# Batch 1's first units scored in one slot each, the values behind the products, and the first output tile summed in another PSUM bank

## The chip, the cores and the metric

The kernel runs on one core of one Trainium2 chip. The metric is device time in microseconds, the median of several executions. Four engines matter here: TensorE (PE) multiplies, with its weight loads (PEld) beside it; ScalarE (ACT) does exponentials and copies; VectorE (DVE) does element-wise work; GpSimd (POOL) does some clamping and issues the loads. SyncE (SP) issues the stores.

## The reference

For 8 batches and 8 heads of 576 positions with head size 64, sliding-window attention with a position bias is computed. The heads of a position are joined to a row of 512. Two matrix products follow, with an ELU between them. Only what fixes the work is kept here:

```python
scores = scale * np.matmul(q, k.transpose(0, 1, 3, 2))
bias = slopes[:, None, None] * (-np.abs(rel))[None]      # rel = query - key position
mask = (rel >= 0) & (rel < 128)
attn = softmax(np.where(mask, scores + bias, -1e9))
x = np.matmul(attn, v).transpose(0, 2, 1, 3).reshape(4608, 512)
h = x @ w_in                                             # 512 -> 2048
g = np.where(h > 0, h, np.exp(np.minimum(h, 0)) - 1)
out = g @ w_out                                          # 2048 -> 512
```

## The kernel before, in words

**One program order, written by hand.** Python lists say what is issued in which *slot*; the loop at the end walks the slots and issues everything, and each engine runs its own part strictly in that order. Within slot `s` the order is: `early`, then the hidden-layer chunk `HID[s]`, then the ELU's last step (`elu`) of the chunk of slot `s - 1`, then the `tasks` of the slot (put there by `at`, or at their head by `at_once`), then the output work `OUT[s]`, then `late` (put there by `after`). A task of `at` thus stands between the hidden chunk and the output products of its slot; one of `after` stands behind the products.

**Attention.** A batch is cut into four units of 128 keys (`u`), and a unit into two halves of four heads. For batches 0 and 1 a half goes through `first_scores` (line 176: four matmuls of 64 rows by 128 columns of the array, 256 wide, two running side by side), `first_expo` (ScalarE, lines 205 and 210), for batch 1 `first_weigh` (VectorE, line 216, the bias and mask as a factor), and later `values` (line 253: the attention times v, then on VectorE a reciprocal `rden`, line 259, and a product `xn`, line 260). `turn` (line 289) transposes `xn` on TensorE and copies it into `xT`, which the hidden layer reads. `turn_first` (line 136) transposes the loaded q and k of a batch into `QT` and `KT`; the loads are those of `s` (line 101). From batch 2 on other functions do this (lines 225 to 285).

**Hidden layer.** A chunk is 16 matmuls of 128 columns (line 305, 32 of 64 columns in some) into a bank `hp0`, `hp1` or `sp2`; then ScalarE takes the exponential (line 315, followed by GpSimd at 316; or lines 312 and 313 on ScalarE alone), and `elu` (VectorE, line 323, `g`) writes `g` and frees the bank.

**Output.** The first 256 rows are summed plainly by `output` (line 329, four 512-wide matmuls per call, four calls per tile of 128 rows; ScalarE copies the sum out at line 336). All later rows go by a scheme of seven products per pair of tiles (`product`, line 393, 256-wide matmuls, 7 or so per slot), with VectorE's `sums` and `combine` (line 354) before and after. For the first pair the products 1, 6, 7 and 4 are summed in bank `op`, and 2, 5 and 3 in `sp3`. `combine(1, "C11")` adds product 2, straight out of `sp3`, to a kept copy of product 1; product 5 then starts over in `sp3`.

**PSUM.** There are eight banks: `sp0` and `sp1` (together `spa`), `sp2`, `sp3`, `hp0`, `hp1`, `av`, `op`. In `first_scores` the argument `d` names a pair of them: `pairs[0]` is `spa`, `pairs[2]` is `hp0` with `hp1`.

```python
for s in range(min(slots), max(slots) + 1):
    for f, a in early.get(s, []):
        f(*a)
    for step in HID.get(s, []):
        hidden(*step, s in SOFT)
    if s - 1 in HID and s not in (1, 4, 5):
        done(s - 1)
    for f, a in tasks.get(s, []):
        f(*a)
    for f, a in OUT.get(s, []):
        f(*a)
    for f, a in late.get(s, []):
        f(*a)
```

Of the kernel before, what the change touches and what calls it, by code (L numbers as in the profile page):

```python
# [18 lines left out]
def kernel(  # L19
# [9 lines left out]
    nc = tc.nc  # L29
# [47 lines left out]
    sp = [spa[:, 0, :], spa[:, 1, :]] + [ps_s.tile([128, 512], F32, name=f"sp{i}", tag=f"sp{i}") for i in (2, 3)]  # L77
    hp = [ps_h.tile([128, 512], F32, name=f"hp{i}", tag=f"hp{i}") for i in range(2)]
    av = ps_v.tile([128, 512], F32, name="av", tag="av")
    op = ps_o.tile([128, 512], F32, name="op", tag="op")  # L80
# [68 lines left out]
    with tc.manual_schedule():  # L149
# [348 lines left out]
        early, tasks, late, HID, OUT = {}, {}, {}, {}, {}  # L498

        def at(s, f, *a):  # L500
            tasks.setdefault(s, []).append((f, a))

        def at_once(s, f, *a):
            tasks.setdefault(s, []).insert(0, (f, a))

        def after(s, f, *a):
            late.setdefault(s, []).append((f, a))
# [23 lines left out]
        for o in range(16 * NTB):  # L531
            t, ts, f = o // 16, o // 4 % 4, o % 4
            if o // 8 in SEVEN:
                continue
            s = (9, 11, 13, 14)[o] if o < 4 else 11 + o if o < 13 else 2 * o - 1 if o < 16 else 15 + o
            OUT[s] = [(output, (t, ts, 4 * f, op))]

        def done(r):
            for step in HID[r]:
# [25 lines left out]
        at(5, first_scores, 0, 3, 1, 0)  # L565
        at(5, first_expo, 0, 3, 1, 0, 0, 256)
        at(5, done, 4)
        at(9, values, 0, 3, 0)
        at(9, values, 0, 3, 1, sp[3])
        at(10, values, 0, 4, 0)  # L570
        at(10, turn, 0, 3, nc.scalar.copy, sp[3])
        at(11, values, 0, 4, 1)
# [12 lines left out]
        at(16, turn_first, 1, 1, 0, 1, sp[3], nc.scalar.copy)  # L585
        at(17, turn_first, 1, 0, 0, 0, hp[1], nc.scalar.copy)
        at(17, turn_first, 1, 0, 0, 1, av, V.tensor_copy)
        at(19, turn_first, 1, 0, 1, 0, av, nc.scalar.copy)
        for u, a0, a1, d in ((0, 18, 19, 2), (1, 20, 21, 2), (2, 22, 24, 0), (3, 26, 28, 0)):
            for half, a in enumerate((a0, a1)):  # L590
                at(a, first_scores, 1, u, half, d * half)
                at(a, first_expo, 1, u, half, d * half, 0, 256)
                at(a + 1, first_weigh, 1, u, half)
                at(a + 2, values, 1, u, half, av if half else sp[2])
            at(a1 + 3 + u // 3, turn, 1, u, nc.scalar.copy, (av, av, av, sp[3])[u])
        at(25, turn_first, 1, 1, 1, 0, av, nc.scalar.copy)
        at(30, values, 1, 4, 0, sp[2])
        at(31, values, 1, 4, 1)
        at(32, turn, 1, 4)
# [6 lines left out]
        for b in range(2, B):  # L606
            for u in range(4):
                a = START[b] + 4 * u
# [11 lines left out]
            a = START[b - 1] if b > 2 else 0  # L620
# [17 lines left out]
        for n in SEVEN:  # L638
            s = 15 + 8 * n
            ps = (19, 20, 21, 22, 23, 25, 27, 29, 30) if n == 1 else range(s, s + 9)  # L640
            if n < 2 * NTB - 1:
                for d, i in ((-1, 1), (1, 2), (3, 3), (4, 4)):
                    (at_once if n > 2 else at)(ps[d] if d > 0 else ps[0] - 1, sums, n, i)
                after(ps[2], combine, n, "C11")
                after(ps[6], combine, n, "C12")
                (at_once if n > 2 else at)(ps[8], combine, n, "C22")
                for d in range(8):
                    OUT[ps[d]] = [(product, (n, i, j, j + 1)) for i, j in turns[7 * d:7 * d + 7]]
            else:
                at_once(s - 3, sums, n, 3)  # L650
                for i in (2, 1):
                    at_once(s - 2, sums, n, i, 0, 6)
                    at_once(s - 1, sums, n, i, 6, 8)
                at(s - 1, product, n, 1)
                OUT[s] = [(product, (n, 2)), (combine, (n, "C11")), (sums, (n, 4)), (product, (n, 6)), (product, (n, 5))]
                OUT[s + 1] = [(product, (n, 7)), (product, (n, 3)), (combine, (n, "C22")), (combine, (n, "C12")),
                              (last_out, (n,))]
# [48 lines left out]
```

## Time and profile before

| | |
|---|---|
| median of three runs | 310.42 us (310.11 to 310.88) |
| profiled execution | 310.72 us, of which the span is 308.9 us |
| granted TensorE clock | 1.00 |
| busy over the span | PE 97%, PEld 83%, DVE 84%, ACT 78%, POOL 35% |
| mean of a 16-matmul hidden chunk, start to start | about 0.89 us |
| `values` half, first unit (4 matmuls) | about 0.11 us |
| line 216 (`first_weigh`) | 0.68 to 0.69 us on DVE |
| line 205 (both banks of `spa`) | 1.02 us on ACT |

The span is from the first instruction to the last; the rest of the 310.72 us lies around it. In a timeline a row gives the start in the span, the duration, the engine, the line, the operation and what is written and read; in brackets stands the engine's idle time before it and what ended that. The rows of TensorE overlap[...]: the time that a group really took is read from one group's start to the next one's start. The slots that the change touches lie between 28 and 70 us.

### The profile page before, as it was taken

How to read it: one execution, taken by the hardware profiler on the slowest of the kernel's cores; microseconds unless marked ns; L12 is line 12 of the kernel's file. 1: busy time of each engine (PE TensorE's matmuls, PEld its weight loads, DVE VectorE, ACT ScalarE, POOL GpSimd, SP SyncE). 2: the span in 40 equal slices, each digit the busy share in tenths (PEclk: the TensorE clock that was granted, in tenths of full speed). 3: DMA queues.
4: the chain of work that ended last, by engine and by line, in shares of the span. 5: the costliest groups of instructions: out<-in, count | busy, mean ns of one | idle time of the engine just before them, and what ended most of it. 6: DMA issues, size and time to landing. Idle time of an engine off the chain costs nothing.

```text
span 308.9 us, 9842 instructions
## 1 busy us (share of the span) xinstructions
PE 300.8 (97%) x4079; PEld 256.5 (83%) x4079; DVE 258.0 (84%) x499; ACT 241.5 (78%) x445; POOL 108.5 (35%) x163
## 2 busy tenths in 40 slices
PE   7899999999999999999999999999999999999996
PEld 5688775798788888988888888888899888888885
DVE  5646887988989999997989998989998788886783
ACT  4576678778889698879797889788988797968881
POOL 8938868274261415140707060806000101010000
PEclk9999999999999999999999999999999999999999
DMA  9999999999197929495979997999620302030103
GB/s 95 188 198 201 201 176 189 92 118 122 23 153 73 152 55 149 55 142 70 109 93 118 130 98 82 125 135 107 68 92 15 96 17 87 19 97 1 70 17 121
DMA packets 96941, 32.04 MB, mean 104 GB/s; under 512 B 83968, under 2 KB 92800, under 8 KB 96896
## 3 DMA queue, kind: packets, MB, share of 16 engines
q0 software_dynamic: 75920, 18.36, 64.8%
q1 hardware_dynamic: 20832, 12.98, 17.4%
q8 instruction: 32, 0.52, 0.7%
q14 instruction: 13, 0.11, 0.1%
q10 hardware_dynamic: 144, 0.07, 0.1%
HBM read 36.70 MB, written 9.44 MB: 149 GB/s over the span
## 4 chain that ended last, share of the span: by engine, by line
PE 76%; DVE 7%; ACT 6%; DMA 5%; issue 3%; POOL 2%; POOLq 0%; DVEq 0%; ACTq 0%
PE hp L305 34%; PE op L393 13%; PE av L393 12%; PE spa L225 4%; PE spa L271 3%; DVE g L323 2%; DMA s<-in_q_dram 2%; DMA VP<-in_v_dram 2%; ACT EX L236 2%; PE op L329 1%; DMA xT<-xn 1%; PE sp L393 1%; POOL e L316 1%; PE sp L305 1%; ACT e L315 1%
## 5 line engine op out<-in xcount | busy, mean ns | idle before, releaser
L305 PE MATMUL hp<-xT,wi 128*128 128x256 f16 (+3 forms) x1488 | 144.2, 245 | 1.2 <-DVE g L323 0.5
L305 PEld LDWEIGHTS <-wi 128*128 128x128 f16 x1600 | 119.7, 98 | 18.2 <-issue 6.1
L323 DVE SCALAR_TENSOR_TENSOR g<-e,hp 128x512 f16<-128x512 f32 x138 | 93.7, 679 | 22.2 <-ACT e L313 12.7
L316 POOL TENSOR_SCALAR e<-e 128x512 f32<-128x512 f32 x44 | 28.0, 635 | 158.9 <-ACT e L315 153.4
L312 ACT ACTIVATE e<-hp 128x512 f32<-128x512 f32 x98 | 58.6, 598 | 28.8 <-PE hp L305 24.3
L313 ACT ACTIVATE e<-e 128x512 f32<-128x512 f32 x100 | 63.1, 631 | 3.2
L393 PEld LDWEIGHTS <-S 128*128 128x128 f16 x544 | 51.2, 98 | 6.8 <-issue 0.6
L393 PEld LDWEIGHTS <-g 128*128 128x128 f16 x400 | 37.4, 98 | 4.6 <-issue 0.6
L241 DVE TENSOR_TENSOR EX<-EX,TAB 128x1024 f16<-128x1024 f16 x48 | 32.9, 686 | 6.1 <-ACT EX L236 4.0
L114 POOL DMA_DIRECT2D VP<-in_v_dram x40 | 34.3, 870 | 0.8 <-PE hp L305 0.3
L315 ACT ACTIVATE e<-hp 128x512 f32<-128x512 f32 x40 | 24.1, 601 | 10.6 <-PE hp L305 10.6
L393 PE MATMUL op<-T,S 128*128 128x256 f16 x200 | 30.0, 273 | 0.1
L233 ACT ACTIVATE EX<-spa 128x1024 f16<-128x1024 f32 x24 | 24.6, 1025 | 3.7 <-PE spa L225 3.4
L393 PE MATMUL av<-T,S 128*128 128x256 f16 x176 | 26.4, 272 | 0.1
L236 ACT ACTIVATE EX<-sp 128x512 f16<-128x512 f32 x48 | 26.0, 596 | 0.0
L354 DVE TENSOR_TENSOR S<-g 128x1024 f16<-128x1024 f16 (+2 forms) x35 | 23.5, 672 | 0.8 <-PE op L393 0.2
L393 PE MATMUL op<-wo,g 128*128 128x256 f16 x128 | 19.2, 272 | 0.1
L393 PE MATMUL av<-wo,g 128*128 128x256 f16 x120 | 18.0, 272 | 0.0
L277 DVE TENSOR_TENSOR xn<-spa,rden 128x512 f16<-128x512 f32 x24 | 16.6, 691 | 0.8
L108 POOL DMA_DIRECT2D st<-in_k_dram x24 | 16.2, 686 | 2.8 <-DMA s<-in_q_dram 1.7
L108 POOL DMA_DIRECT2D st<-in_q_dram x24 | 15.9, 666 | 0.8 <-DMA VP<-in_v_dram 0.7
L271 PE MATMUL spa<-VP,EX 128*128 128x65 f16 x336 | 15.3, 193 | 0.1
(139 smaller groups left out, 382.5 us busy)
## 6 DMA issues: line engine op xcount, KB each, us to landing
out_dram<-ob SPq DMA_DIRECT2D x32, 256.0 KB, 2.8
VP<-in_v_dram POOLq DMA_DIRECT2D x32, 128.0 KB, 5.7
st<-in_k_dram POOLq DMA_DIRECT2D x24, 144.0 KB, 5.2
st<-in_q_dram POOLq DMA_DIRECT2D x24, 144.0 KB, 6.3
wi<-in_moe_w_in_dram POOLq DMA_DIRECT2D x4, 512.0 KB, 11.1
wo<-in_moe_w_out_dram POOLq DMA_DIRECT2D x4, 512.0 KB, 9.7
out_dram<-ob SPq DMA_DIRECT2D x7, 128.0 KB, 1.7
VP<-in_v_dram POOLq DMA_DIRECT2D x8, 64.0 KB, 5.9
```

Source lines behind the costliest of these rows:

```text
L108: nc.gpsimd.dma_start(st[b][32 * g:32 * g + 32, w, :, :, :, :].rearrange("p h n j d -> p (h n) (j d)"), (q, k)[w][b, 2 * g:2 * g + 2, :, : ...
L114: nc.gpsimd.dma_start(VP[b % 2][0:p, n, :, 0:D], v[b, :, 128 * n:128 * n + p, :].rearrange("h p d -> p h d"))
L233: nc.scalar.activation(unit(b, u)[:, 0:2, :, :], spa.rearrange("p g (h c) -> p g h c", h=2), AF.Exp, scale=0.125)
L236: nc.scalar.activation(unit(b, u)[:, g, :, :], sp[g].rearrange("p (h c) -> p h c", h=2), AF.Exp, scale=0.125)
L241: V.tensor_tensor(out=e, in0=e, in1=TAB[:, int(u == 3), 2 * gp:2 * gp + 2, :, :], op=ALU.mult)
L305: nc.tensor.matmul(p[:, l * w + u0:l * w + u1], w_in_sb[:, c, fc * 128:(fc + 1) * 128], xT[:, c, x0:x0 + u1 - u0], start=(c == 0), stop=(c ...
L312: nc.scalar.activation(e[:, 0:n], p[:, 0:n], AF.Relu, scale=-1.0)
L313: nc.scalar.activation(e[:, 0:n], e[:, 0:n], AF.Exp, scale=-1.0)
L315: nc.scalar.activation(e[:, 0:n], p[:, 0:n], AF.Exp)
L316: nc.gpsimd.tensor_scalar(out=e[:, 0:n], in0=e[:, 0:n], scalar1=1.0, scalar2=0.0, op0=ALU.min, op1=ALU.max)
L323: V.scalar_tensor_tensor(out=gs[t][:, f0:f0 + nf, c0:c0 + w], in0=sh(es.pop((t, c0, f0))), scalar=1.0, in1=sh(hps.pop((t, c0, f0))), op0=A ...
L393: nc.tensor.matmul(o, a[:, j, :], b[:, j, :], start=j == 0 and i in (1, 2, 5), stop=j == 7, skip_group_check=True)
```

## The change

Three things are moved. The values of unit 3 of batch 0 go from slot 9 to slot 8. The sum of the first output tile goes from bank `op` to `sp0`. In batch 1 the second parts of k and q are transposed in slot 17 along with the first; units 0 and 1 are scored with both halves in one slot (18 and 20), behind the output work; their values, the first turn and the first half of unit 2 go behind the products too; and the turns of units 0 to 2 stand in slots 22 (late), 25 and 27. `sums(1, 2)` moves to the head of its slot.

```diff
-            OUT[s] = [(output, (t, ts, 4 * f, op))]
+            OUT[s] = [(output, (t, ts, 4 * f, op if ts else sp[0]))]
...
-        at(9, values, 0, 3, 0)
-        at(9, values, 0, 3, 1, sp[3])
+        at(8, values, 0, 3, 0)
+        at(8, values, 0, 3, 1, sp[3])
...
         at(17, turn_first, 1, 0, 0, 0, hp[1], nc.scalar.copy)
         at(17, turn_first, 1, 0, 0, 1, av, V.tensor_copy)
-        at(19, turn_first, 1, 0, 1, 0, av, nc.scalar.copy)
-        for u, a0, a1, d in ((0, 18, 19, 2), (1, 20, 21, 2), (2, 22, 24, 0), (3, 26, 28, 0)):
+        at(17, turn_first, 1, 1, 1, 0, sp[3], nc.scalar.copy)
+        at(17, turn_first, 1, 0, 1, 0, sp[2], nc.scalar.copy)
+        for u, a in ((0, 18), (1, 20)):
+            for half in range(2):
+                after(a, first_scores, 1, u, half, 2 * half)
+                after(a, first_expo, 1, u, half, 2 * half, 0, 256)
+                at(a + 1 + half, first_weigh, 1, u, half)
+                if (u, half) != (1, 0):
+                    after(a + 2 + half, values, 1, u, half, av if half else sp[2])
+        after(22, turn, 1, 0, nc.scalar.copy, av)
+        for u, a0, a1 in ((2, 22, 24), (3, 26, 28)):
             for half, a in enumerate((a0, a1)):
-                at(a, first_scores, 1, u, half, d * half)
-                at(a, first_expo, 1, u, half, d * half, 0, 256)
+                (after if a == 22 else at)(a, first_scores, 1, u, half, 0)
+                (after if a == 22 else at)(a, first_expo, 1, u, half, 0, 0, 256)
                 at(a + 1, first_weigh, 1, u, half)
                 at(a + 2, values, 1, u, half, av if half else sp[2])
-            at(a1 + 3 + u // 3, turn, 1, u, nc.scalar.copy, (av, av, av, sp[3])[u])
-        at(25, turn_first, 1, 1, 1, 0, av, nc.scalar.copy)
+        after(22, values, 1, 1, 0, sp[2])
+        at(25, turn, 1, 1, nc.scalar.copy, av)
+        at(27, turn, 1, 2, nc.scalar.copy, av)
+        at(32, turn, 1, 3, nc.scalar.copy, sp[3])
...
-                    (at_once if n > 2 else at)(ps[d] if d > 0 else ps[0] - 1, sums, n, i)
+                    (at_once if n > 2 or n == 1 and i == 2 else at)(ps[d] if d > 0 else ps[0] - 1, sums, n, i)
```

## The prediction

> **What bounds the kernel now.** First the page's busy shares and the table of windows: TensorE is the engine without slack, and its granted clock is full everywhere.
>
> ```profile
> PE 300.8 (97%) x4079; PEld 256.5 (83%) x4079; DVE 258.0 (84%) x499; ACT 241.5 (78%) x445; POOL 108.5 (35%) x163
> 40.00:50.00 10.00, 9.62 (x174) 6.59 (x172) 8.26 (x12) 7.82 (x13) 6.22 (x11) 1.00 2.14 177
> 50.00:60.00 10.00, 9.51 (x127) 6.92 (x122) 8.75 (x22) 7.58 (x15) 4.49 (x7) 1.00 1.61 147
> ```
>
> The columns of a window are its length, then the busy time of PE, PEld, DVE, ACT and POOL, the clock, and the DMA columns. PE leaves only 0.4 to 0.5 us idle per 10 us there, but weight loads drop to 6.6 and 6.9: its records cover waits. So I read the timeline next, from start to start, with 0.89 us for a hidden chunk, 0.107 us for a 256-wide matmul (seven in 60.68 to 61.45) and 0.22 us for four turns.
>
> ```profile
> 28.46 1.06 PE L305 MATMUL hp<-xT,wi 128*128 128x128 f16 x16
> 29.84 1.05 PE L305 MATMUL hp<-xT,wi 128*128 128x128 f16 x16 [0.32 <-DVE g L323]
> ...
> 40.17 1.06 PE L305 MATMUL hp<-xT,wi 128*128 128x128 f16 x16
> 40.73 0.57 ACT L336 COPY ob<-op 128x512 f32<-128x512 f32 x1
> 41.34 1.02 PE L329 MATMUL op<-wo,g 128*128 128x512 f16 x4
> ```
>
> The chunk at 28.46 should end at 29.35, yet the next starts at 29.84, when VectorE has freed `hp1`: 0.49 lost. The chunk at 40.17 ends at 41.06; the second tile's sum starts at 41.34, when ScalarE has copied the first out of `op`: 0.28 lost.
>
> ```profile
> 51.93 0.82 PE L393 MATMUL sp<-wo,g 128*128 128x256 f16 x6
> 52.15 0.68 DVE L216 TENSOR_TENSOR EX<-EX,TAB 128x1024 f16<-128x1024 f16 x1
> 52.88 0.30 PE L253 MATMUL av<-VP,EX 128*128 128x65 f16 x4
> ...
> 54.49 0.41 DVE L354 TENSOR_TENSOR ob<-U,sp 128x256 f32<-128x256 f32 x1
> ...
> 59.11 0.39 PE L176 MATMUL spa<-QT,KT 64*128 64x256 f16 x4
> 59.43 0.90 PEld L305 LDWEIGHTS <-wi 128*128 128x128 f16 x16 [0.21 <-issue]
> ```
>
> Six products from 51.93 end at 52.57; the values start at 52.88, right after the weighing they read: 0.31 lost. In the same way 0.32 goes at 48.47 (the first scores, behind ScalarE's q copy of 47.42), 0.18 at 50.50 (`op`, behind the second tile's copy), 0.21 at 54.64 and 0.31 at 56.39 (values behind weighings), 0.25 at 57.32 (product 7 behind its sum). With the first two that is 2.35 us of waits. Besides, the half unit at 59.11 needs 0.21 (four matmuls, two side by side) and takes 0.33; the chunk behind it takes 0.99 for 0.89. Each change of the array's shape costs about 0.11.
>
> **What the Trainium skill says.** *TensorEngine Tiling (Array Packing)*, Key Properties: changing the tiling mode drains the engine. The trace agrees: 0.11 per change. *TensorE: Matmul & The Clock Gate*, "Architectural detail", says that ScalarE and VectorE are strict FIFO; every order here follows that. *PSUM — Partial Sum Buffer*, "PSUM bank collisions", asks that engines be kept apart by bank: hence the wait of 41.34, a new sum waiting for an old one's copy.
>
> **The change part by part.** I walk it forward on the timeline's own times. POOL and SP keep the same instructions in the same sequence, so no load or store passes another; loads move only with their issuers.
>
> *Slots 8 to 16.* The 16 value matmuls of unit 3 (30.73 to 31.22 now, 0.49 us) fit into the 0.49 wait at 29.35. Their inputs are there (the exponentials ended at 27.8, `sp3` was read by 26.5). On VectorE their four instructions (1.2 us) pass in front of the `g` that frees `hp0`, which slips from 30.88 to about 31.7; `hp0` is wanted at about 32.95, so that is covered; with that cover gone each us would cost one. Gain 0.49. The first tile's sum in `sp0` leaves `op` free: gain 0.28. `spa` is last read at 27.8 and wanted again in slot 18, after the copy near 40.3, so nothing new waits. Both are on PE's path: it stands 0.77 ahead, at 45.38 instead of 46.15 for slot 17's transposes.
>
> *Slot 17.* The transposes end at 46.39 (47.16 - 0.77). The two second parts follow: 16 take 0.45 (eight took 49.76 to 50.01, a part of a drain among it), and one drain, to 46.95. Their data landed at 43.1 and 44.9, counted from issue (35.35, 36.89) by the landing times of 7.8 and 8.0. Their two copies on ScalarE (0.41 and 0.38) go between the q copy and the output copy, where it would idle. Drain and two output groups (1.73) run to 48.78, covering the 0.32 wait for the q copy. Both halves of unit 0: one drain and 0.43, to 49.31.
>
> *Drains.* From slot 17 to 25 there were 15 changes of shape, now 9: six times 0.11, 0.65 us less PE work.
>
> *Slots 18 to 22, where the change adds waits.* ScalarE copies the second tile from 48.99 (a record ends 0.17 behind its last column) to 49.56, and product 1 starts at 49.6: a wait of 0.2, as at 50.50 before. Fourteen products run to 51.1. The exponential of `spa` runs 49.48 to 50.50, the weighing 50.53 to 51.21, the values 51.26 to 51.37, unit 1's first half (drain, 0.21) to 51.69. ScalarE's next: two exponentials to 51.5, product 1's copy to 51.8, then `spa` of unit 1, 51.9 to 52.92. VectorE weighs that at 52.96, does the second half's `rden` and `xn` (0.56), and only then C11, 54.12 to 54.53. PE meanwhile did 0.21 of scores, a drain, ten products and four values, and is ready at 53.2 for product 5 in `sp3`, which C11 must read first. **It waits about 1.35 us.** Before, C11 ended at 54.90 and product 5 began only at 55.65; C11 was hidden. Queued behind this wait are the first turn, unit 2's scores and values (1,1,0), product 7 and slot 24's chunk; ScalarE waits for turn and scores, VectorE for its exponential.
>
> *Slots 22 to 27.* Product 5 starts at 54.57, four take 0.43, the turn 0.22, ScalarE copies from 55.43 and takes unit 2's exponential 55.92 to 56.94; the weighing starts at 57.0. Behind it VectorE does, start to start, weighing 0.60, sum 0.61, two `rden`/`xn` pairs 1.12, transpose 0.36, `g` 0.64, weighing 0.60, transpose 0.59 and `g` 0.69: that frees `hp0` at 62.2. Slot 27's chunk can start at 62.25; before, its first column went in at about 63.05 (its row starts at 63.01, with the rest of a drain in it). **The walk gives 0.8 us.** From there instructions, durations and waits are as before, and the later waits (69.90, 78.10) hang on the same neighbours, so I carry 0.8 to the end. PE's removed waits and drains (2.35 + 0.65) thus come back only in part: VectorE's order is late next.
>
> Against its own 310.72 (span 308.9 and 1.8 around it) that is 309.9; against the median 310.42, which is 0.3 lower, 309.6. What the trace doesn't show is how close the handovers of slots 18 to 22 come in the new order. I bound them from 0.4 us sooner to 0.7 later, and take the walk's value.
>
> **The rivals.** *VectorE's late C11 costs half.* If the exponentials and weighings of slots 18 to 22 interlock tighter than walked, product 5 waits 0.7 and not 1.35; all behind it follows, and the gain is about 1.45: 309.0. For it: VectorE idled 0.7 at 50.9 before, and drains are gone. Against: each handover above is taken from a row. *Slower.* The second parts now stand in front of PE's first scores in slot 17, wanted at 46.4. Should one land after 48.2 instead of 44.9, scores, exponentials and C11 move with it one for one; 1.8 us late turns the 0.8 into a loss of 1 and more: 311.6. For it: loads of 512 KB took 11.8 us, these of 64 KB took 8. Against: 1.5 us of slack and an unchanged POOL order. *No gain at all*: if C11 comes 0.8 later, 310.4, within the bound. That the change does nothing is excluded: the built order shows every move.
>
> **How the numbers follow.** 0.3% is 0.93 us, about what a measurement of this kernel can tell from no change. The walk and its neighbours, a gain of 0 to 0.93, get 0.54; the tighter interlock beyond 0.93 gets 0.34; slower 0.12, most of it handovers or loads that I misjudge. The likeliest alone reaches from 309.5 to 310.4; the range goes to 308.9 for the tighter case and 310.8 for a small loss.
>
> **What would show it.** In the profile after: no wait in front of slot 9's chunk nor of the second tile's first group; two halves of `L176` in one run with one drain each side, twice; a gap of over 1 us in front of `sp<-T,S` with C11 (`ob<-U,sp`) ending it; and slot 27's chunk near 62.2. The prediction is wrong if product 5 doesn't wait, if slot 17's transposes wait for a load, or if the 0.8 at 62 us isn't there at the end.

## The result and the profile after

| | before | after |
|---|---|---|
| median of six runs | 310.33 us (310.09 to 310.88) | 309.05 us (308.68 to 309.61) |
| ratio | | 0.995 (0.9929 to 0.9972) |
| profiled execution | 310.72 us, span 308.9 | 309.05 us, span 307.2 |

The changed kernel is 1.28 us faster, 0.4%. That lies inside the range (308.9 to 310.8) but outside the likeliest case: the walk gave 0.8 us, and a gain of up to 0.93 us (0.3%) was called the likeliest.

First the busy line and the two windows of the profile after; the columns are as before.

```profile
PE 299.3 (97%) x4079; PEld 256.6 (84%) x4079; DVE 257.6 (84%) x499; ACT 241.5 (79%) x445; POOL 108.8 (35%) x163
40.00:50.00 10.00, 9.62 (x180) 7.05 (x178) 7.61 (x11) 7.67 (x14) 6.21 (x10) 1.00 2.02 178
50.00:60.00 10.00, 8.82 (x132) 7.27 (x130) 9.52 (x24) 7.62 (x14) 6.57 (x9) 1.00 1.76 156
```

The counts of the whole run are the same. In the second window PE idles 1.18 us where it idled 0.49, and yet it loads weights for 7.27 us in place of 6.92. The natural reading is that waits that lay inside records have become one open wait. VectorE is at 9.5 of 10.

The timeline of after, in the order of the prediction's steps (rows in between that play no part are left out, here and in the timelines below):

```profile
27.22 1.06 PE L305 MATMUL hp<-xT,wi 128*128 128x128 f16 x16
28.11 0.41 PE L253 MATMUL av<-VP,EX 128*128 128x65 f16 x8
28.36 0.40 PE L253 MATMUL sp<-VP,EX 128*128 128x65 f16 x8
28.60 1.05 PE L305 MATMUL hp<-xT,wi 128*128 128x128 f16 x16
...
38.45 1.06 PE L305 MATMUL hp<-xT,wi 128*128 128x128 f16 x16
39.00 0.57 ACT L336 COPY ob<-spa 128x512 f32<-128x512 f32 x1
39.34 1.03 PE L329 MATMUL op<-wo,g 128*128 128x512 f16 x4
```

From the chunk of slot 8 to that of slot 9 there are 1.38 us as before (28.46 to 29.84), but now they hold slot 8's chunk and the values, and no bracket stands at 28.60. The second tile's first group starts at 39.34, 0.89 behind its chunk (38.45), where before it was 1.17 (40.17 to 41.34).

```profile
44.15 0.64 PE L136 MATMUL hp<-ident,s 128*64 128x128 f16 x16
44.62 0.61 PE L136 MATMUL av<-ident,s 128*64 128x128 f16 x16
45.16 0.31 PE L136 MATMUL sp<-ident,s 64*64 64x64 f16 x8
45.72 0.31 PE L136 MATMUL sp<-ident,s 64*64 64x64 f16 x8 [0.25 <-DMA s<-in_q_dram]
45.97 1.90 PE L329 MATMUL op<-wo,g 128*128 128x512 f16 x8
47.80 0.39 PE L176 MATMUL spa<-QT,KT 64*128 64x256 f16 x4
48.03 0.38 PE L176 MATMUL hp<-QT,KT 64*128 64x256 f16 x4
...
52.52 0.18 DVE L259 RECIPROCAL rden<-av 128x4 f32<-128x4 f32 x1
52.74 0.42 DVE L260 TENSOR_TENSOR xn<-av,rden 128x256 f16<-128x256 f32 x1
53.08 0.41 DVE L354 TENSOR_TENSOR ob<-U,sp 128x256 f32<-128x256 f32 x1
...
53.54 0.60 PE L393 MATMUL sp<-T,S 128*128 128x256 f16 x4 [1.18 <-DVE ob L354]
60.37 0.69 DVE L323 SCALAR_TENSOR_TENSOR g<-e,hp 128x512 f16<-128x512 f32 x1
61.11 1.05 PE L305 MATMUL hp<-xT,wi 128*128 128x128 f16 x16 [0.15 <-DVE g L323]
```

Slot 17 has a new bracket: eight of the 16 narrow transposes wait for the second part of q. Both halves of `L176` stand in one run. Product 5 waits 1.18 us and C11 (`ob<-U,sp`) ends it, behind the `rden` and `xn` of 52.52. Slot 27's chunk (61.11) follows `g`. In before, product 5 and slot 27's chunk had stood without a bracket:

```profile
55.65 0.60 PE L393 MATMUL sp<-T,S 128*128 128x256 f16 x4
63.01 1.07 PE L305 MATMUL hp<-xT,wi 128*128 128x128 f16 x16
```

These times can't be laid on those of before directly: something had moved ahead of all of them. The first row of q's transposes shows it, before and then after:

```profile
8.29 0.44 PE L136 MATMUL hp<-ident,s 64*64 64x64 f16 x16 [1.04 <-DMA s<-in_q_dram]
```

```profile
7.04 0.44 PE L136 MATMUL hp<-ident,s 64*64 64x64 f16 x16 [0.32 <-DMA s<-in_q_dram]
```

The first load of q was issued at 2.47 us in both. It landed 1.24 us earlier in after, and the chunk of slot 8 also starts 1.24 earlier (28.46 against 27.22). Nothing that the change touches has run by then. The load is not all of it: the k transposes ahead of it, which in before wait for no load, start at 6.00 in before and at 5.48 in after. So "on before's clock" below means after's time plus 1.24: slot 27's chunk is at 62.35, against 63.01.

To follow the gain I took, from both traces, the end of each hidden chunk, counted from the end of slot 8's chunk. The gain of after is 0.49 us after slot 9's chunk, 0.76 after slot 16's, 0.54 at slot 24's, 0.68 from slot 27 on and 0.50 at the last. The profiled difference of 1.74 us at the last instruction is thus 1.24 ahead of the change and 0.50 behind it.

Stated theory for the experiments: the two small parts give 0.77, the rest a little, and the load's wait takes part of that back; the early start is a matter of the execution. Rivals: the start belongs to the changed program; or the 1.28 us are the changed slots alone.

### The profile page after: what moved, and what is told of

It reads as the page before. It is cut to its first block, busy times and chain, and to the rows that moved or that the text cites. A ratio compares the mean times of both kernels' runs of the same rounds, so it can differ in the third digit from the quotient of the medians.

```text
span 307.2 us, 9841 instructions
## 1 busy us (share of the span) xinstructions
PE 299.3 (97%) x4079; PEld 256.6 (84%) x4079; DVE 257.6 (84%) x499; ACT 241.5 (79%) x445; POOL 108.8 (35%) x163
## 4 chain that ended last, share of the span: by engine, by line
PE 77%; DMA 6%; ACT 5%; DVE 5%; POOL 3%; issue 2%; POOLq 0%; DVEq 0%; ACTq 0%
PE hp L305 35%; PE op L393 13%; PE av L393 13%; PE spa L225 4%; DMA s<-in_q_dram 3%; PE spa L271 3%; DMA wi<-in_moe_w_in_dram 2%; PE sp L393 2%; DVE g L323 2%; ACT e L315 2%; PE sp L253 1%; ACT EX L236 1%; POOL e L316 1%; POOL VP L114 1%; PE sp L305 1%
## 5 line engine op out<-in xcount | busy, mean ns | idle before, releaser
L315 ACT ACTIVATE e<-hp 128x512 f32<-128x512 f32 x40 | 24.0, 601 | 10.6 <-PE hp L305 10.6
```

Of the source, the lines that this page charges most:

```text
L315: nc.scalar.activation(e[:, 0:n], p[:, 0:n], AF.Exp)
```

## Experiments

Each kernel ran on the chip beside the kernel before. "Gain from slot 8" is the measure of the last paragraphs, in that kernel's profile against before's.

**How far one trace repeats.** The two kernels, unchanged, were run again, in the first set of experiments and once more in later ones.

> The kernel before, unchanged, against itself: ratio 1.000 in every theory. What tells theories apart is its timeline up to 15 us, which the change doesn't touch. In the profiled run of before the first q load landed at 8.24 us and the first hidden chunk started at 13.61; in that of after 7.00 and 12.66. Theory 1 (the change gives 0.8 us where the walk puts it, and the two profiled runs differ by luck in that load): here the landing falls anywhere between 7 and 8.3 us. Theory 2 (the change, by what it does to the program, lets the first loads land earlier): it lands at 8.2 again.

> The changed kernel once more. Theory 1: ratio 0.9974 (0.8 us), the first result of 1.3 us being 0.5 us of luck; the first q load lands anywhere between 7 and 8.3 us. Theory 2: the 1.3 us is the change's own, ratio 0.996 again, and the first q load lands near 7.0 us again.

> The kernel before, unchanged, once more. Ratio 1.000. First q landing 7.8 to 8.3 if its time belongs to the program; anywhere from 7.0 if it is luck.

> The changed kernel a third time, for its start. Theory 1 (start is luck): first q landing 7.8 to 8.3 is as likely as 7.0; from slot 8 on (last chunk of the span against the chunk before slot 8's) it gains 0.5 to 1.1 us on before, by how long slot 17's transposes wait for their load. Theory 3 (an earlier start belongs to this program): 7.0 a third time. Ratio 0.997 by theory 1, 0.996 by theory 3.

| | median, runs | ratio to before | q landed (profile) | gain from slot 8, slots 27 on |
|---|---|---|---|---|
| before_again | 310.25, 14 | 1.001 (0.999 to 1.0031) | 8.12 | -0.01 |
| before_third | 309.75, 14 | 1.0005 (0.9984 to 1.0027) | 8.05 | about 0 |
| after_again | 309.12, 11 | 0.9974 (0.9951 to 0.9996) | 7.04 | 0.87 |
| after_third | 309.12, 16 | 0.9964 (0.9947 to 0.9981) | 7.12 | 0.61 |

From slot 8 on the three executions of before agree to 0.02 us, but for 0.3 us between 100 and 108 us that are back by 109. So outside that stretch the gain by chunk can be read to hundredths; after's own three differ, by the length of slot 17's wait. The start repeats by program: early in each profile of after, late in each of before. The timeline of after_third:

```profile
7.16 0.44 PE L136 MATMUL hp<-ident,s 64*64 64x64 f16 x16 [0.30 <-DMA s<-in_q_dram]
...
45.90 0.31 PE L136 MATMUL sp<-ident,s 64*64 64x64 f16 x8 [0.32 <-DMA s<-in_q_dram]
```

The load's wait is there again, at the same place. The medians of the three comparisons of after with before differ by 1.28, 0.76 and 1.06 us.

**The two small parts alone (early_two).** The kernel before with two edits:

```diff
-            OUT[s] = [(output, (t, ts, 4 * f, op))]
+            OUT[s] = [(output, (t, ts, 4 * f, op if ts else sp[0]))]
...
-        at(9, values, 0, 3, 0)
-        at(9, values, 0, 3, 1, sp[3])
+        at(8, values, 0, 3, 0)
+        at(8, values, 0, 3, 1, sp[3])
```

> The kernel before with two parts of the change alone: batch 0's fourth values in slot 8 and the first tile's sum in sp0. Both theories: the waits at 29.84 (0.49 us) and 41.34 (0.28 us) are gone and nothing new waits: 0.6 to 0.8 us faster, ratio 0.9975. Rival: the loads of batch 1 set the pace of slots 16 to 24 by the clock, so TensorE's lead is given back at a load's landing: ratio above 0.999.

Measured: 309.21 us (22 runs), ratio 0.9975 (0.9961 to 0.999), which is 0.8 us by the ratio. From slot 8 the gain is 0.49 at slot 9 and 0.76 from slot 16 to the end. The timeline:

```profile
29.41 1.06 PE L305 MATMUL hp<-xT,wi 128*128 128x128 f16 x16
30.30 0.41 PE L253 MATMUL av<-VP,EX 128*128 128x65 f16 x8
...
40.64 1.06 PE L305 MATMUL hp<-xT,wi 128*128 128x128 f16 x16
41.53 1.03 PE L329 MATMUL op<-wo,g 128*128 128x512 f16 x4
```

No brackets, and 0.89 from the chunk (40.64) to the sum (41.53). With all of batch 1 as before, these two parts go through to the end whole.

**The rest of the change alone (batch1_alone).** After, with those two edits undone.

> The kernel before with the rest of the change alone (batch 1's transposes, scores, values and turns moved, sums(1,2) at the head), the values of batch 0 and the first tile's bank as before. By the walk product 5 waits over 1 us for C11 and slot 27's chunk is only 0.2 us (0 to 0.3) earlier than before: ratio 0.9993. Rival, that this part is worth the half of the 1.3 us measured: 0.65 us, ratio 0.998, with the wait for C11 under 0.8 us.

Measured: 309.86 us (22 runs), ratio 0.9994 (0.998 to 1.0008), which doesn't tell it from no change. The trace does: the gain from slot 8 is 0.35 us, a little above the 0 to 0.3 expected and below the rival's 0.65. Its timeline:

```profile
54.88 0.41 DVE L354 TENSOR_TENSOR ob<-U,sp 128x256 f32<-128x256 f32 x1
55.35 0.38 PE L393 MATMUL sp<-T,S 128*128 128x256 f16 x2 [1.18 <-DVE ob L354]
```

The same wait of 1.18 us, without the small parts and without a wait for a load. 0.76 and 0.35 make 1.11: what the whole should give where the load doesn't hold it up.

**The wait for the load (after_loads).** After, with the second parts of k and q loaded earlier.

```diff
-        at(11, load_first, 1, 1, 1)
-        at(12, load_first, 1, 0, 1)
+        at(10, load_first, 1, 1, 1)
+        at(10, load_first, 1, 0, 1)
```

> The changed kernel with the loads of batch 1's second k and q parts issued in slot 10, in front of the five v loads and not between them. If slot 17's transposes wait for the second q load (0.44 us in the profile after, 0.25 in the repeat, none with the long warm-up), that wait is gone: from slot 8 on the gain is 1.1 us whatever the start. Nothing else should move; v lands later but is wanted only in slot 20. Rival: the wait is not the load's, and the gain stays between 0.5 and 0.9.

Measured: 309.17 us (22 runs), ratio 0.9966 (0.9953 to 0.9979). The loads landed at 42.28 and 43.03 instead of 44.05 and 45.67 in after. The timeline of slot 17:

```profile
45.64 0.44 PE L136 MATMUL sp<-ident,s 64*64 64x64 f16 x16
46.01 1.90 PE L329 MATMUL op<-wo,g 128*128 128x512 f16 x8
```

All 16 transposes in one run, no bracket, 0.37 us from row to row where after took 0.81 (45.16 to 45.97): the load cost 0.44 there. The gain from slot 8 is 1.11 at slot 27, the sum of the two parts. At the end it is 0.85, against after_third's 0.55; so the expected 1.1 is there at 62 us and not wholly at the end. The medians of the two, 309.17 and 309.12 on the same chip, don't show these 0.3 us.

**The wait for C11 (c11_first).** After, with C11 at the head of slot 21's `late`, ahead of the reciprocal and product of the second half of unit 0.

```diff
-                after(ps[2], combine, n, "C11")
+                (late.setdefault(ps[2], []).insert(0, (combine, (n, "C11"))) if n == 1 else after(ps[2], combine, n, "C11"))
```

> The changed kernel with one thing moved: in slot 21 VectorE does combine C11 ahead of the reciprocal and product of values (1,0,1), 0.56 us earlier in its queue. If C11 holds product 5, as the profile after shows (product 5 at 53.54, C11 from 53.08), the wait of 1.2 us falls to about 0.6 and slot 27's chunk and the end come 0.3 to 0.5 us earlier than after. Rival: slot 27 hangs on VectorE's total work, of which this moves nothing: the end as in after.

Measured: 308.74 us (11 runs), ratio 0.9954 (0.9936 to 0.9973). The timeline:

```profile
53.62 0.69 DVE L216 TENSOR_TENSOR EX<-EX,TAB 128x1024 f16<-128x1024 f16 x1
54.23 0.41 DVE L354 TENSOR_TENSOR ob<-U,sp 128x256 f32<-128x256 f32 x1
54.56 0.18 DVE L259 RECIPROCAL rden<-av 128x4 f32<-128x4 f32 x1
54.69 0.60 PE L393 MATMUL sp<-T,S 128*128 128x256 f16 x4 [0.63 <-DVE ob L354]
```

C11 now precedes `rden`, right behind a weighing; the wait falls from 1.18 to 0.63 us, and the gain from slot 8 rises to 1.54, which is 0.43 more than the 1.11 above. So 0.43 of the 0.55 us taken from this wait come back, at slot 27 and at the end: VectorE's order is on the path. This profile has no wait for a load: its start was late (q at 8.14), and the second q landed 1.3 us ahead of its transposes.

**Both (c11_loads).** After with both edits.

> Both: C11 ahead of (1,0,1)'s reciprocal, and the two loads in slot 10. From slot 8 on 1.5 us gained whatever the start (c11_first alone: 1.54 with a late start, where the load didn't bind; 1.2 or less would be expected of it with an early one). Ratio about 0.995.

Measured: 308.54 us (9 runs), ratio 0.9944 (0.9919 to 0.9969), 309.12 and 310.18 for after and before on the same chip. The gain from slot 8 is 1.54, as in c11_first. The timeline:

```profile
8.32 0.44 PE L136 MATMUL hp<-ident,s 64*64 64x64 f16 x16 [0.82 <-DMA s<-in_q_dram]
...
53.37 0.41 DVE L354 TENSOR_TENSOR ob<-U,sp 128x256 f32<-128x256 f32 x1
53.84 0.60 PE L393 MATMUL sp<-T,S 128*128 128x256 f16 x4 [0.63 <-DVE ob L354]
```

It has the lowest median of all. Its interval overlaps with that of after. Against before it is shown faster; against after, the shorter wait is shown and a shorter total is not.

**A start that doesn't hang on the load (before_longwarm, after_longwarm).** Both kernels with more matmuls ahead of the first transposes, so that these find q landed in either kernel.

```diff
-        warm(22)
+        warm(60)
```

> The kernel before with 60 warming matmuls ahead of the first transposes in place of 22, so that TensorE comes to the first q transposes after that load has landed (about 8.3 us at the latest) and with its clock granted. 1 to 2 us slower than before. If the spread of the runs comes from that load and the clock, it becomes smaller. First q landing: 7.8 to 8.2 if its time belongs to the program, as in before, before_again and early_two; anywhere between 7.0 and 8.3 if it is luck.

> The changed kernel with 60 warming matmuls. Both start at the same time now, so the difference to before_longwarm is that of the changed slots alone. Theory 1: 0.8 us (0.6 to 1.0), of which product 5's wait for C11 keeps over 1 us back. Theory 2, that the changed slots are worth 1.3: 1.2 to 1.4. Theory 3, that an earlier start belongs to the changed program: 0.8 here, and the first q landing is at 7.0 again.

Measured: 315.06 us, ratio 1.015 (1.0126 to 1.0174), and 314.68 us, ratio 1.014 (1.0111 to 1.0168), six runs each: about 5 us slower, not 1 to 2, and only 0.4 us apart. For the totals this experiment failed. The end of slot 8's chunk is 3.2 us later than in before's profile in before_longwarm and 3.5 in after_longwarm, and one or two waits far from here add the rest, 1.7 us in before_longwarm and 2.7 in after_longwarm. One of them, in the latter's timeline:

```profile
120.21 0.72 PE L305 MATMUL hp<-xT,wi 128*128 128x64 f16 x12 [1.14 <-DMA xT<-xn]
```

A hidden chunk waits for a transpose that a DMA makes, which in after's own profile no chunk does. With these waits after_longwarm's lead is gone at the end. Up to the first of them the trace is of use. Its timeline in slot 17:

```profile
49.88 0.44 PE L136 MATMUL sp<-ident,s 64*64 64x64 f16 x16
50.25 1.90 PE L329 MATMUL op<-wo,g 128*128 128x512 f16 x8
```

Again no wait for a load, 0.37 us for the transposes, and a gain from slot 8 of 0.76 at slot 16 and 1.12 at slot 27: after_loads' values, from another edit. That lies between the 0.6 to 1.0 of the first theory and the 1.2 to 1.4 of the second. The first q landed at 8.03 and 8.10, so with the long warm-up the changed program has no early landing, against the third theory.

## Why the prediction was wrong, and where it was right

The total failed: 0.8 us was walked and up to 0.93 called the likeliest, and 1.28 was measured. Two steps of the walk failed, with opposite signs: the term for slot 17's transposes (0.67 us in place of 0.37), and the slack of the loads (1.5 us, in place of waits of 0.25 to 0.51). A third thing was left out, the start. The first two are shown. In after's profile they nearly cancel, so they alone do not make 1.28 of 0.8; how the timed 1.28 divides between slots and start is not shown.

**Right: the first two steps.** "Gain 0.49" and "gain 0.28" were measured as 0.49 and, together, 0.76; early_two brought them to the end undiminished. On before's clock the transposes of slot 17 ended at 46.40 (the narrow ones' row at 45.16), where the prediction has 46.39.

**Right: the wait for C11.** "It waits about 1.35 us" was 1.18. That VectorE's order holds back what TensorE saved was shown by c11_first. The strict order within VectorE that the Trainium skill states (*TensorE: Matmul & The Clock Gate*, "Architectural detail") is what this experiment used: the instruction put in front is the one that ends the wait. The rival with a wait of 0.7 us did not come true, though its total (a gain of 1.45) lies nearer to the timed 1.28.

**Wrong in size: slot 17.** The prediction counted from the row at 46.39 "0.45" for 16 narrow transposes, "and one drain", and then another drain ahead of the output groups: 0.67 us to their row. Measured is 0.37 from row to row (after_longwarm, after_loads). The 0.45 was scaled from a row that, as the prediction itself says, had part of a drain in it, and the start of the row at 46.39 seems to hold one as well: of the two groups of 16 wide transposes ahead of it the first takes 0.47 (44.15 to 44.62), the one next to the change of shape 0.54 (44.62 to 45.16). The term is 0.3 us too long, everything down to `g` hangs on it, and without a wait for the load slot 27's chunk comes 1.1 us earlier and not 0.8. The Trainium skill says that a change of tiling mode drains the engine (*TensorEngine Tiling (Array Packing)*, Key Properties); the runs show the whole stretch, and not the 0.11 each and the 0.65 in all.

**Wrong: "1.5 us of slack" for the loads.** The prediction took the landings of before as they stood. In after the second q was issued at 35.17, 1.72 earlier than before, and landed at 45.67, 0.81 later: 10.5 us in place of 8.0; and by the early start TensorE came for it 1.24 us sooner than walked. TensorE waited for it, the mechanism of the slower rival, for 0.44, 0.25 and 0.51 us in the three profiles of after, far from the 1.8 that this rival put on it. after_loads and after_longwarm show the same transposes without it. Together with the term above this nearly cancels: 62.35 for slot 27's chunk on before's clock, predicted 62.25. That agreement is luck.

**Right in part: what is there at 62 us goes to the end.** early_two kept 0.76 of 0.76, c11_first 1.54 of 1.55. The profiles of after kept 0.50 of 0.68, 0.86 of 0.87 and 0.55 of 0.61; after_loads lost the most, 1.11 to 0.85. Why these lose some is not shown.

**Missing: the start.** The prediction took everything before slot 8 as given. In the three profiles of after slot 8's chunk ends 1.24, 0.75 and 1.13 us sooner than in the first profile of before, and in before's other two 0.86 and 0.79 later. By the trace the changed slots are worth 0.5 to 0.9 us at the end in a run with the early start and its load wait.

The timed runs put this in proportion. Before's median was 310.33 in the first comparison, from six runs, and 309.88, 309.98 and 310.18 in the later ones, from 56, 24 and 40; that of after was 309.05, 309.12 and 309.12. So 0.15 to 0.45 of the first 1.28 us is a difference between before and before. And the profiled execution of before, 310.72, lies 0.5 to 0.8 above those later medians, while the profiled ones of after (309.05, 309.19 and 309.17) lie at after's. As the profiles of before agree from slot 8 to the end, a usual run of before starts, by estimate, 0.5 to 0.8 us sooner than the first profiled one did: so much of the 1.24 us belongs to that execution and not to the change.

**What stays open.** How much of the timed gain is the start's: 0.76 to 1.06 us in the larger comparisons, less the 0.5 to 0.9 of the traces, leaves anything from nothing to 0.6. Open too is why the profiled starts differ. The early landing (7.0 to 7.1) is in all profiles of after and after_loads, the late one (7.8 to 8.3) in all others, c11_first and c11_loads among them. c11_first differs from after by the place of C11 alone, at 53 us, so the moved parts alone do not bring the early landing about. For early_two, batch1_alone, c11_first and c11_loads, where q lands late as in before, the timed gains by the ratio (0.8, 0.2, 1.4, 1.7 us) fit those of the traces (0.76, 0.35, 1.54, 1.54). The 1.1 us at slot 27 are shown for after_loads and after_longwarm, and not for after as it was timed.

## What to carry to other kernels

When two traces are laid side by side, find the first row that differs before reading any gain, and count the gain from the last point that the change can't have touched. A row behind a change of array shape may already hold the drain: take durations from row to row in a place with the same neighbours. And in these runs a load issued earlier on a busy queue did not land earlier by as much: slack for a transfer has to be counted with the traffic that it meets in the new order. Last, take the profiled execution's own total and see where it lies among the timed runs before its start is taken for a usual one.

## What the hardware showed that I had not expected

- The second q (64 KB), as long as its place among the loads stays, lands almost regardless of when it is issued. In before's three profiles and early_two it was issued at 36.9 to 37.8 us and took 7.5 to 8.0; in the three of after, issued at 35.2 to 35.7, it took 10.3 to 10.6; in batch1_alone and c11_first, issued at 37.1 and 37.3, it took 9.1 and 8.7. All nine landings lie between 44.9 and 46.2 us. With its place moved to the front of the v loads (after_loads, c11_loads) it landed at 43.0 and 43.3, from issue at 33.9 and 34.7. In before's profile the 16 DMA engines were about 90% busy or more in that stretch.
- A lower granted clock between 5 and 15 us goes with a total about 2 us longer. In the profiled execution of before_third it was 0.85 from 5 to 10 us and 0.80 from 10 to 15, in that of before 1.00, and 1.00 from 15 us on in both; their totals are 311.49 and 310.72. Of the 14 runs of before_third nine lie at 309.46 to 310.08, with a mean clock of 1.00, and five at 311.46 to 312.04, with 0.993 or 0.994. A median of few runs can move by this more than by the change.
- A later start is not a mere shift. With slot 8's chunk 4.7 us later in after_longwarm than in after, two DMA transposes (issued at 116.09 and 132.77 us) took 4.08 and 4.28 us, where the same two had taken 2.42 and 2.44, and chunks that had not waited for them waited 1.14 and 1.55. Why they took longer is not shown.
